# Token rows of a retention and mixture-of-experts kernel, moved into the quadrants of the matmul array

## The chip, the cores and the metric

One core of a Trainium2 chip runs the whole program. The metric is the device time of one launch in microseconds (us), lower is better. The kernel before took 1379.56 us in the median of three runs (1375.28 to 1381.71).

## What is computed

Eight batches of 576 tokens go through a retention layer with eight heads of 64 (scores, a decay mask by head, no softmax), then through eight experts, each token through the one with its largest gate product, and then through a second layer with a cosine. The reference, cut to what matters:

```python
ret = scale * np.matmul(q, k.transpose(0, 1, 3, 2)) * Dmat      # Dmat = gamma[h] ** (i - j), i >= j
x = np.matmul(ret, v)                     # (8, 8, 576, 64), then (4608, 512): a token's heads side by side
logits = x @ w_gate                       # (4608, 8)
expert_idx = np.argmax(logits, axis=1)
for e in range(8):
    mask = expert_idx == e
    out[mask] = gate_w[mask, None] * (np.maximum(x[mask] @ w1[e], 0.0) @ w2[e])
h = out @ w_in
result = (h * np.cos(h)) @ w_out
```

## The kernel before, in words

The program has three stages: attention with routing (to about 175 us), the experts, and the cosine layer. The change touches the first and the host's layout of two inputs.

The first stage walks 40 steps: eight batches, each in five chunks of tokens (four of 128, one of 64; `CH`). The loop `for i in range(NS)` emits instructions in the order in which the engines run them; there is no scheduler behind it, each engine works through its own list in order. The step numbers differ by function: step i does `scores(i)`, `decay(i + 1)`, `inter(i - 1)`, `intra(i - 1)` and `rows(i - 2)`.

- `load` (lines 438 to 441) brings transposed k and q, and v and k by rows: 1 MB for a full chunk, 384 KB for a half one. Five buffers; step i issues the load of step i + 4 on SyncE's queue, behind the store of token rows of that step.
- `decay` (L449) scales the values by head: eight ScalarE multiplications of 128x64 into `vs`.
- `scores` (L462): 16 TensorE matmuls of 64x64 weights by 128 columns, in the four quadrants of the array (two heads by two halves of the keys). VectorE multiplies the two PSUM banks by the causal mask into `pT` (L466).
- `inter` (L487) multiplies q by the sum carried from earlier chunks (`sbd`), `intra` (L497) the masked scores by the values; both add into `xps`. VectorE scales the sum into `xt` (L500). L506 adds the chunk to the carried sum, which ScalarE copies to `sbd` (L509).
- `rows` (L518) turns the transposed result into token rows and takes the gate products at once: four matmuls with 128x128 of `xt` as weights and 136 columns of `wgi`, an identity (128) beside the gate weights (8). ScalarE copies the rows to `xs` (L520), VectorE adds up two pairs' gate products (L521), and SyncE stores the rows to `xd` (L523).
- `route`, `place`, `spread` and `table` work once a batch: the token's expert (VectorE), its place among the expert's tokens (small matmuls L555 to L563), a one-hot spread on GpSimd (L575 to L626), and a matmul that enters it into the token table (L637). The GpSimd part begins in the third step of the next batch, and the table matmul stands behind `intra` three steps later.

In a trace a float32 matmul stands as two records, so 16 matmuls read x32. The scores, the rows and the turned expert inputs share four PSUM banks ("sc").

At the start, 13 bf16 matmuls on a blank tile (`warm`) come first. GpSimd makes the decay tables of chunks 1 to 4 (L399) and issues three small DMAs for the gate weights, from which `setup_rows` builds `wgi` on VectorE.

Of the kernel before, what the change touches and what calls it, by code (L numbers as in the profile page):

```python
# [22 lines left out]
P = 128  # L23
# [17 lines left out]
NWARM = 13  # L41

# [19 lines left out]
C_EYE = C_BASE + E  # L62
C_LO = C_EYE + E
# [5 lines left out]
def const_table(B):  # L69

    NT = B * SEQ
    t = np.zeros((P, C_END), np.float64)
    p = np.arange(P)
    t[:, C_ID:C_ID + 128] = np.eye(128)
    t[:, C_MASK:C_MASK + 128] = p[:, None] <= p[None, :]
    t[:, C_TRI:C_TRI + 128] = p[:, None] < p[None, :]
    t[:, C_ONE:C_ONE + 128] = 1.0
    t[:, C_IOTA:C_IOTA + 128] = p
    gam = 1.0 - 2.0 ** (-5.0 - np.arange(H))

    hp = 2 * np.arange(4)[None, :] + ((p >= D)[:, None] ^ (np.arange(4) % 2 == 1)[None, :])
    for c, (o, n) in enumerate(CH):
        pos = (o + p)[:, None] - CENTER
        t[:, C_GK + c * H:C_GK + (c + 1) * H] = gam[None] ** (-pos)
        t[:, C_GF + 4 * c:C_GF + 4 * c + 4] = gam[hp] ** o
        t[:, C_REV + c * E:C_REV + (c + 1) * E] = E - np.arange(E)
    t[:, C_GX:C_GX + 512] = (gam[hp][:, :, None] ** (p - CENTER)[None, None, :] / math.sqrt(D)).reshape(P, 512)
    t[0, C_BASE:C_BASE + E] = NT * np.arange(E)
    for j in range(4):
        t[32 * j:32 * j + E, C_EYE:C_EYE + E] = np.eye(E)  # L90
    t[:, C_B:C_B + MAXOVB] = np.arange(MAXOVB)
    t[:, C_E:C_E + E] = np.arange(E)
    t[:, C_WIN:C_WIN + E] = WIN
    for e in range(E):
        t[:, C_LO + e * NBLK:C_LO + (e + 1) * NBLK] = e * NT + P * np.arange(NBLK)
    for c in range(NBLK):
        t[:, C_SLOT + c] = c * P + p
    for b in range(B):
        for c, (o, n) in enumerate(CH):
            t[:, C_TOK + b * NCH + c] = b * SEQ + o + p  # L100
    return t.astype(np.float32)


def of_chunks(q, k, v):
# [13 lines left out]
    return full, np.concatenate([turned(k, o, n), turned(q, o, n)], axis=2), rows(v, o, n)  # L118


@with_exitstack
def attn_moe_kernel(ctx, tc, full, part, tail, wg, w1, w2, win, wout, ctab, out):
# [235 lines left out]
    with ExitStack() as actx:  # L358
# [16 lines left out]
        wgs = ap1.tile([P, 4, E], F32, name="wgs")  # L375

        RW = P + E
# [11 lines left out]

        def setup_rows():  # L390
            nc.vector.tensor_copy(out=wgi[:, 0::2, 0:P], in_=ident.unsqueeze(1).to_broadcast([P, 2, P]))
            for a in range(2):
                nc.vector.tensor_copy(out=wgi[:, 1::2, a * D:(a + 1) * D],
                                      in_=ident[:, (1 - a) * D:(2 - a) * D].unsqueeze(1).to_broadcast([P, 2, D]))
            nc.vector.tensor_copy(out=wgi[:, :, P:RW], in_=wgs)
# [47 lines left out]
        def decay(i):  # L443
            b, c = steps[i]
            o, n = CH[c]
            s = st[i]
            vs = ap3.tile([P, H, D], F32, tag="vs", name="vs", bufs=4) if n == P else halfv[b % 2]
            for h in range(H):
                nc.scalar.mul(vs[:n, h], s["v"][:n, h], cc(C_GK + c * H + h, 1, n))  # L449
            s["vs"] = vs  # L450
# [60 lines left out]
        def rows(i):  # L511
            b, c = steps[i]
            o, n = CH[c]
            x = ap3.tile([P, 4, P], F32, tag="xs", name="xs")
            for g in range(2):
                two = ps1.tile([P, 4, P], F32, tag="sc", name="rw", bufs=4).rearrange("p (j a) t -> p j (a t)", a=2)
                for j in range(2):
                    mm(out=two[:, j, 0:RW], lhsT=xts[i % 3][:, 2 * g + j, :], rhs=wgi[:, 2 * g + j, :], start=(j == 0),  # L518
                       stop=True, skip_group_check=True)
                nc.scalar.copy(out=x[:n, 2 * g:2 * g + 2], in_=two[:n, :, 0:P])  # L520
                nc.vector.tensor_reduce(out=lgt[b % 2][:n, c, g, :], in_=two[:n, :, P:RW].rearrange("p j e -> p e j"),  # L521
                                        axis=AX.X, op=ALU.add)
            nc.sync.dma_start(out=xd[b * SEQ + o:b * SEQ + o + n, :], in_=x[:n].rearrange("p j t -> p (j t)"))  # L523
# [175 lines left out]

        load(0, (0, 2))  # L700
        nc.sync.dma_start(out=ca[:, :C_TRI - C_MASK], in_=ctab[:, C_MASK:C_TRI])
        load(0, (2, 3))
        load(1, (0, 2))
        nc.sync.dma_start(out=gx[:, 0].rearrange("p j t -> p (j t)"), in_=ctab[:, C_GX:])
        load(0, (3, 4))
        load(1, (2, 4))
        load(2, (0, 2))
        nc.sync.dma_start(out=ct, in_=ctab[:, :C_MASK])
        load(2, (2, 4))
        load(3)  # L710
        wgc = wg.rearrange("(c p) e -> p c e", p=P)
        nc.gpsimd.dma_start(out=wgs[:, 0::2], in_=wgc[:, 0::2])
        for a in range(2):
            nc.gpsimd.dma_start(out=wgs[a * D:(a + 1) * D, 1::2], in_=wgc[(1 - a) * D:(2 - a) * D, 1::2])
# [4 lines left out]
        warm(NWARM, ps1.tile([P, 8, P], F32, tag="x", name="xps").rearrange("p a t -> p (a t)"), idle)  # L719
        decay(0)  # L720
# [3 lines left out]
        for i in range(NS):  # L724
# [6 lines left out]
            if i + 1 < NS:  # L731
                decay(i + 1)
            if i == 1:
                setup_rows()
# [13 lines left out]
            if i >= 2:  # L748
                rows(i - 2)
# [24 lines left out]

        inter(NS - 1)
        intra(NS - 1)
        rows(NS - 2)
# [656 lines left out]
```

## Time and profile before

| | |
|---|---|
| median of 3 runs | 1379.56 us |
| the profiled execution | 1377.58 us, its span 1375.3 us |
| TensorE busy (share of the span) | 1354.1 us (98%) |
| VectorE busy | 939.5 us (68%) |
| ScalarE busy | 757.2 us (55%) |
| GpSimd busy | 191.0 us (14%) |
| HBM traffic over the span | 217 GB/s |

Busy shares are means over three stages with different limits. A profile of a stage is read from windows of time, and a wait from the rows around it: a bracket behind a row says how long its engine stood idle before it and what released it.

### The profile page before, as it was taken

The page shows a single profiled execution, that of the slowest core. Times are in us where ns is not written, and L with a number is a line of the kernel's source. Part 1 is how long each engine was busy: PE and PEld are TensorE (multiplying, and loading weights), DVE is VectorE, ACT ScalarE, POOL GpSimd, SP SyncE. Part 2 cuts the span into 40 slices and gives each one's busy share as a digit, 9 for nine tenths or more (in the row PEclk, how much of TensorE's full clock was granted, in tenths as well). Part 3 has the DMA queues.
Part 4 walks back from the last instruction along what each step waited for, and adds up shares of the span by engine and source line. Part 5 has one row for each costly group of instructions (what it writes and reads, how often), then busy time and mean ns, then how long its engine had stood idle before and what let it go on. Part 6 is the DMA issues. An engine that isn't in the chain of part 4 may idle for free.

```text
span 1375.3 us, 28314 instructions
## 1 busy us (share of the span) xinstructions
PE 1354.1 (98%) x11234; PEld 1262.5 (92%) x11234; DVE 939.5 (68%) x1928; ACT 757.2 (55%) x1687; POOL 191.0 (14%) x300
## 2 busy tenths in 40 slices
PE   7999999999999999999999999999999999999998
PEld 6888899999999999998999999999999999999997
DVE  4777865867778687847666676766767676666655
ACT  5788725444544455336556555555555555555544
POOL 4334530121211212100010100101001010010101
PEclk9999999999999999999999999999999999999999
DMA  8899626575876668976564655646455564564551
GB/s 290 320 329 346 213 61 217 180 262 183 285 246 203 211 230 268 331 275 259 176 258 164 220 190 191 220 166 249 183 192 201 194 233 161 209 226 162 196 184 57
DMA packets 72648, 300.58 MB, mean 219 GB/s; under 512 B 7748, under 2 KB 15904, under 8 KB 58560
## 3 DMA queue, kind: packets, MB, share of 16 engines
q1 hardware_dynamic: 60000, 256.18, 53.0%
q0 software_dynamic: 12512, 42.56, 8.3%
q8 instruction: 89, 1.46, 0.4%
q14 instruction: 47, 0.39, 0.1%
HBM read 247.24 MB, written 51.47 MB: 217 GB/s over the span
## 4 chain that ended last, share of the span: by engine, by line
PE 49%; issue 6%; POOL 0%; POOLq 0%; ACT 0%
PE acc L1341 25%; PE hps L1265 24%; POOL out_dram L1323 0%; POOLq L1430 0%; ACT ka L1295 0%; POOL spare L159 0%; PE acc L1352 0%; POOLq L1323 0%; ACT orow L1321 0%
## 5 line engine op out<-in xcount | busy, mean ns | idle before, releaser
L1341 PE MATMUL acc<-wunit,gh 128*128 128x512 f32 x1152 | 358.2, 392 | 0.0
L1265 PEld LDWEIGHTS hps<-far,wquad 128*128 128x128 f32 x2064 | 261.8, 191 | 8.0 <-ACTq L1239 0.7
L1265 PE MATMUL hps<-far,wquad 128*128 128x256 f32 x2064 | 266.7, 283 | 0.5 <-ACTq L1239 0.5
L1341 PEld LDWEIGHTS acc<-wunit,gh 128*128 128x128 f32 x1152 | 207.2, 189 | 36.0
L1341 PE MATMUL acc<-wunit,gl 128*128 128x512 f32 x576 | 224.3, 389 | 0.0
L274 PE MATMUL hps<-xT,wunit 128*128 128x256 f32 (+6 forms) x1536 | 209.4, 297 | 0.5 <-ACT yev L291 0.5
L274 PEld LDWEIGHTS hps<-xT,wunit 128*128 128x128 f32 x1536 | 206.7, 188 | 0.9 <-ACT yev L291 0.7
L289 PE MATMUL hps<-hh,wunit 128*128 128x256 f32 (+6 forms) x960 | 197.9, 301 | 0.0
L289 PEld LDWEIGHTS hps<-hh,wunit 128*128 128x128 f32 x960 | 155.8, 190 | 0.1
L289 PE MATMUL hps<-hl,wunit 128*128 128x256 f32 (+6 forms) x480 | 143.5, 299 | 1.4 <-DVE hl L278 1.4
L1323 POOL DMA_INDIRECT out_dram<-orow,perm x36 | 35.4, 982 | 740.3 <-DVE orow L1319 736.4
L1341 PEld LDWEIGHTS acc<-wunit,gl 128*128 128x128 f32 x576 | 108.2, 188 | 24.5 <-DVE gl L1308 0.8
L1306 ACT CAST gh<-sa 128x512 fp32r<-128x512 f32 x144 | 89.6, 622 | 72.9 <-DVE sa L1302 72.9
L1302 DVE SCALAR_TENSOR_TENSOR sa<-sa,box 128x512 f32<-128x512 f32 x144 | 99.0, 688 | 42.8 <-ACT sa L1300 41.7
L1265 PE MATMUL hps<-near,wquad 128*128 128x256 f32 x960 | 126.6, 283 | 0.0
L1265 PEld LDWEIGHTS hps<-near,wquad 128*128 128x128 f32 x960 | 123.1, 191 | 3.6
L1276 DVE TENSOR_TENSOR box<-hps,box 128x256 f32<-128x256 f32 x72 | 30.6, 424 | 136.7 <-PE hps L1265 136.5
L1308 DVE TENSOR_TENSOR gl<-sa,gh 128x512 fp32r<-128x512 f32 x144 | 98.9, 687 | 18.5 <-ACT gh L1306 12.9
L1297 DVE SCALAR_TENSOR_TENSOR sa<-box,ka 128x512 f32<-128x512 f32 x144 | 98.9, 687 | 12.4 <-ACT ka L1295 12.3
L1275 ACT COPY box<-hps 128x256 f32<-128x256 f32 x72 | 26.8, 372 | 141.3 <-PE hps L1265 132.5
L1021 DVE TENSOR_TENSOR wunit<-wst,wunit 128x512 fp32r<-128x512 f32 x112 | 75.2, 686 | 36.9 <-ACT wunit L1020 36.8
L1299 ACT ACTIVATE sa<-sa 128x512 f32<-128x512 f32 x144 | 91.2, 634 | 8.6 <-DVE sa L1297 8.6
(217 smaller groups left out, 1877.4 us busy)
## 6 DMA issues: line engine op xcount, KB each, us to landing
wquad<-ws SPq DMA_DIRECT2D x72, 1792.0 KB
wst<-in_moe_w_dram SPq DMA_DIRECT2D x64, 512.0 KB
ld<-in_full_dram SPq DMA_DIRECT2D x29, 1024.0 KB
ws<-cvo POOLq DMA_DIRECT2D x28, 512.0 KB, 3.5
xd<-xs SPq DMA_DIRECT2D x32, 256.0 KB
cvw<-in_moe_w_in_dram SPq DMA_DIRECT2D x16, 512.0 KB
cvw<-in_moe_w_out_dram SPq DMA_DIRECT2D x16, 512.0 KB
wd<-cvo POOLq DMA_DIRECT2D x16, 512.0 KB, 5.3
```

What stands on the lines that cost most here:

```text
L274: mm(out=ph[:, :n], lhsT=u[:, a, kc, f0:f0 + P], rhs=t[:, bq, kc, :n], start=(idx == 0), stop=(idx == 11))
L289: mm(out=py[:, :n], lhsT=u[:, w], rhs=t[:, :n], start=(fc == 0 and g == 0), stop=(fc == 7 and g == 2))
L1021: nc.vector.tensor_sub(out=u[:, 1, 2 * g + c], in0=s[:, c], in1=u[:, 0, 2 * g + c])
L1265: mm(out=o, lhsT=u[:, s, kc, a], rhs=x[:, bq, kc], start=(s in (0, 1, 2) and idx == 0), stop=(idx == 5), skip_group_check=True)
L1276: nc.vector.tensor_add(out=u2, in0=y[:, :HT], in1=p1)
L1297: nc.vector.scalar_tensor_tensor(out=sa, in0=x, scalar=INV2PI, in1=ka, op0=ALU.mult, op1=ALU.subtract)
L1299: nc.scalar.activation(out=sa, in_=sa, func=AF.Sin, scale=math.pi)
L1302: nc.vector.scalar_tensor_tensor(out=sa, in0=sa, scalar=-1.0, in1=x, op0=ALU.add, op1=ALU.mult)
L1306: nc.scalar.copy(out=gh, in_=sa)
L1308: nc.vector.tensor_sub(out=gl, in0=sa, in1=gh)
L1323: ins = nc.gpsimd.indirect_dma_start(out=out[:, :], out_offset=bass.IndirectOffsetOnAxis(ap=perm[:, k:k + 1], axis=0), in_=o, in_offset=None)
L1341: mm(out=acc2[T][c], lhsT=pair[n][:, fh, c % 2 * P:(c % 2 + 1) * P], rhs=u[:, w, fc % 4], start=(q == 0 and fh == 0 and n == 0 and w == 0) ...
```

## The change

`rows` uses the array in quadrants: for each of four head pairs, two halves of the features and two halves of the tokens, one matmul of 64x64 by 72 columns (64 of an identity, 8 of gate weights); a PSUM bank now holds one half of the features for all four pairs, so a gate product adds four numbers instead of two. It is emitted between `scores` and `inter` of a step, no longer behind `intra`. The gate table with its identities comes from the host in one DMA on SyncE's queue; `setup_rows` and the three small DMAs go. The tokens' features change order within odd pairs, and the host orders the gate's and w1's rows to match.

`decay`: in the first three steps one VectorE multiplication of 128x512 does all heads, emitted behind the step's own scores; from step 3 on ScalarE does heads 0 to 3 one by one and GpSimd heads 4 to 7 in one multiplication. At the start a ScalarE multiplication of one element comes first (it brings the table load forward), the loads are reordered, and six more warming matmuls stand behind the first scores.

```diff
+def of_gate(w):
+    t = w.reshape(4, 2, D, E).copy()
+    t[1::2] = t[1::2, ::-1]
+    out = np.zeros((2, D, 4, RW), w.dtype)
+    out[:, :, :, :D] = np.eye(D)[:, None, :]
+    out[:, :, :, D:] = t.transpose(1, 2, 0, 3)
+    return out.reshape(P, 4 * RW)
...
-            for h in range(H):
+            h0 = 0 if i < OWN else H // 2
+            for h in range(h0):
                 nc.scalar.mul(vs[:n, h], s["v"][:n, h], cc(C_GK + c * H + h, 1, n))
+            (nc.vector if i < OWN else nc.gpsimd).tensor_tensor(
+                out=vs[:n, h0:], in0=s["v"][:n, h0:],
+                in1=cc(C_GK + c * H + h0, H - h0, n).unsqueeze(2).to_broadcast([n, H - h0, D]), op=ALU.mult)
...
         def rows(i):
-            x = ap3.tile([P, 4, P], F32, tag="xs", name="xs")
+            xt = xts[i % 3]
+            x = ap3.tile([P, 4, 2, D], F32, tag="xs", name="xs")
+            two = [ps1.tile([P, 4, P], F32, tag="sc", name="rw", bufs=4).rearrange("p j t -> p (j t)")[
+                :, :4 * RW].rearrange("p (j f) -> p j f", f=RW) for g in range(2)]
+            for j in range(4):
+                for g, r in ((0, 0), (1, D), (0, D), (1, 0)):
+                    if r < n:
+                        mm(out=two[g][r:r + D, j, :], lhsT=xt[D * g:D * g + D, j, r:r + D],
+                           rhs=wgi[D * g:D * g + D, j, :], start=(j == 0), stop=True, skip_group_check=True)
             for g in range(2):
-                two = ps1.tile([P, 4, P], F32, tag="sc", name="rw", bufs=4).rearrange("p (j a) t -> p j (a t)", a=2)
-                for j in range(2):
-                    mm(out=two[:, j, 0:RW], lhsT=xts[i % 3][:, 2 * g + j, :], rhs=wgi[:, 2 * g + j, :], start=(j == 0),
-                       stop=True, skip_group_check=True)
-                nc.scalar.copy(out=x[:n, 2 * g:2 * g + 2], in_=two[:n, :, 0:P])
-                nc.vector.tensor_reduce(out=lgt[b % 2][:n, c, g, :], in_=two[:n, :, P:RW].rearrange("p j e -> p e j"),
+                nc.scalar.copy(out=x[:n, :, g, :], in_=two[g][:n, :, 0:D])
+                nc.vector.tensor_reduce(out=lgt[b % 2][:n, c, g, :], in_=two[g][:n, :, D:RW].rearrange("p j e -> p e j"),
                                         axis=AX.X, op=ALU.add)
...
+        nc.scalar.mul(spare, one[0:1], one[0:1])
         load(0, (0, 2))
         nc.sync.dma_start(out=ca[:, :C_TRI - C_MASK], in_=ctab[:, C_MASK:C_TRI])
+        load(1, (0, 2))
         load(0, (2, 3))
-        load(1, (0, 2))
+        load(0, (3, 4))
         nc.sync.dma_start(out=gx[:, 0].rearrange("p j t -> p (j t)"), in_=ctab[:, C_GX:])
-        load(0, (3, 4))
         load(1, (2, 4))
         load(2, (0, 2))
+        nc.sync.dma_start(out=wgi.rearrange("p c e -> p (c e)"), in_=wg)
...
-        decay(0)
...
             scores(i)
-            if i + 1 < NS:
+            if i < OWN:
+                decay(i)
+            if i == 0:
+                warm(NWARM // 2, blank, idle)
+            if OWN <= i + 1 < NS:
                 decay(i + 1)
-            if i == 1:
-                setup_rows()
+            if i >= 2:
+                rows(i - 2)
...
             if i >= 1:
                 inter(i - 1)
                 intra(i - 1)
...
-            if i >= 2:
-                rows(i - 2)
```

TensorE's list in the third step, before: scores, carried sum (`sbd`), within the chunk (`pT`, `vs`), sum `S`, rows (`rw`), and the next scores.

```order
L462 MATMUL sc<-ld 64x128 x16
L487 MATMUL xps<-ld,sbd_136 64x128 x8
L497 MATMUL xps<-pT,vs 64x128 x8
L506 MATMUL S<-vs,ld 64x64 x8
L518 MATMUL rw<-wgi,xt_130 128x136 x4
```

The same step after the change:

```order
L474 MATMUL sc<-ld 64x128 x16
L533 MATMUL rw<-wgi,xt_129 64x72 x16
L499 MATMUL xps<-ld,sbd_135 64x128 x8
L509 MATMUL xps<-pT,vs 64x128 x8
L518 MATMUL S<-vs,ld 64x64 x8
```

The rows moved from the step's end to behind its scores, and four matmuls became 16.

GpSimd's list around a batch's spread, before (`dd`, `hot`, `rt`, `oh` lead to the token table):

```order
L584 TENSOR_TENSOR dd<-dd,hot 128x200
L608 TENSOR_SCALAR tokc<-ct 128x5
L609 TENSOR_TENSOR rt<-hot,tokc 128x5x40
L612 TENSOR_SCALAR oh<-ca,rm 128x128 x5
L626 TENSOR_TENSOR rt<-hot,gh 128x5x40
L626 TENSOR_TENSOR rt<-hot,gl 128x5x40
```

And after, where `vs` and `halfv` are the scaled values:

```order
L600 TENSOR_TENSOR dd<-dd,hot 128x200
L459 TENSOR_TENSOR halfv_142<-ld,ca 64x256
L624 TENSOR_SCALAR tokc<-ct 128x5
L625 TENSOR_TENSOR rt<-hot,tokc 128x5x40
L628 TENSOR_SCALAR oh<-ca,rm 128x128 x5
L642 TENSOR_TENSOR rt<-hot,gh 128x5x40
L642 TENSOR_TENSOR rt<-hot,gl 128x5x40
L459 TENSOR_TENSOR vs<-ld,ca 128x256 x4
```

One multiplication now stands in the middle of the chain and four stand between one batch's chain and the next.

## Rows read from the trace of the kernel before

**Rows 1.** The page: busy time by engine, and the chain that ended last
```profile
PE 1354.1 (98%) x11234; PEld 1262.5 (92%) x11234; DVE 939.5 (68%) x1928; ACT 757.2 (55%) x1687; POOL 191.0 (14%) x300
...
PE 49%; issue 6%; POOL 0%; POOLq 0%; ACT 0%
```
**Rows 2.** Windows: length, busy PE, PEld, DVE, ACT, POOL, granted clock, DMA share, GB/s
```profile
0.00:21.23 21.23, 13.41 (x198) 10.79 (x198) 6.04 (x16) 9.85 (x36) 14.97 (x32) 0.92 0.86 294
89.99:109.78 19.79, 19.54 (x405) 17.68 (x404) 15.73 (x47) 16.54 (x59) 8.52 (x16) 1.00 0.92 326
109.78:129.48 19.70, 19.70 (x406) 17.75 (x405) 15.72 (x47) 16.31 (x59) 8.34 (x15) 1.00 0.96 351
129.48:148.97 19.49, 19.49 (x406) 17.70 (x405) 15.92 (x51) 16.18 (x59) 8.14 (x15) 1.00 0.88 306
...
85.00:90.00 5.00, 5.00 (x92) 4.43 (x88) 4.30 (x14) 4.18 (x14) 4.67 (x9) 1.00 1.04 406
...
166.00:1375.30 1209.30, 1198.92 (x8121) 1123.88 (x8121) 823.82 (x1578) 632.24 (x1236) 121.87 (x177) 1.00 0.58 206
```
**Rows 3.** Timeline, one full step, weight loads: start, us, engine, line, operation, [idle before]
```profile
102.04 0.86 PEld L462 LDWEIGHTS sc<-ld 64*64 64x64 f32 x32
102.86 0.48 PEld L487 LDWEIGHTS xps<-ld,sbd 64*64 64x64 f32 x16
103.51 0.85 PEld L497 LDWEIGHTS xps<-pT,vs 128*64 128x64 f32 x16 [0.17 <-issue]
105.00 0.99 PEld L518 LDWEIGHTS rw<-wgi,xt 128*128 128x128 f32 x8
106.12 0.20 PEld L462 LDWEIGHTS sc<-ld 64*64 64x64 f32 x4
```
**Rows 4.** Timeline of TensorE at a half chunk
```profile
110.71 0.41 PE L487 MATMUL xps<-ld,sbd 64*64 64x64 f32 x16
111.05 0.69 PE L497 MATMUL xps<-halfpT,halfv 128*64 128x64 f32 x16
111.68 0.55 PE L637 MATMUL lg<-rt,oh 128*128 128x120 f32 x3
```
**Rows 5.** Timeline of one spread on GpSimd; a table matmul a batch earlier
```profile
102.98 0.52 POOL L575 TENSOR_TENSOR dd<-dsts,ca 128x200 f32<-128x200 f32 x1 [10.85 <-DVE dsts L569]
...
110.17 0.53 POOL L626 TENSOR_TENSOR rt<-hot,gh 128x200 fp32r<-128x200 f32 x1
110.65 0.97 POOL L626 TENSOR_TENSOR rt<-hot,gl 128x200 fp32r<-128x200 f32 x1
...
92.19 0.91 PE L637 MATMUL lg<-rt,oh 128*128 128x120 f32 x5 [0.25 <-POOL rt L626]
```
**Rows 6.** Timeline of the start, TensorE and ScalarE
```profile
1.15 2.95 PE L211 MATMUL xps<-idle 128*128 128x256 bf16 x13 [1.15 <-DVE idle L718]
9.88 1.98 PE L462 MATMUL sc<-ld 64*64 64x128 f32 x32 [3.44 <-DMA ld<-in_full_dram]
18.02 0.67 PE L487 MATMUL xps<-ld,sbd 64*64 64x128 f32 x16 [2.68 <-ACT sbd L509]
...
8.51 1.28 ACT L449 ACT_TABLE_LOAD   x1 [8.51 <-DMA ld<-in_full_dram]
...
18.98 2.02 ACT L449 ACTIVATE vs<-ld,ca 128x64 f32<-128x64 f32 x8 [1.01 <-DMA ld<-in_full_dram]
```
**Rows 7.** Waits (20 to 166 us), the long stall, VectorE by form, a DMA queue
```profile
ACT vs L449 <- DMA ld<-in_full_dram: 13.6, 12, 3.6
...
60.46 1.78 ACT L449 ACTIVATE vs<-ld,ca 128x64 f32<-128x64 f32 x7 [3.57 <-DMA ld<-in_full_dram]
60.85 0.39 PE L506 MATMUL S<-vs,ld 128*64 128x64 f32 x6 [1.67 <-issue]
...
L500 DVE TENSOR_TENSOR xt<-xps,gx 128x512 f32<-128x512 f32 x13 | 8.8, 676 | 0.0
...
q8 instruction: 22, 0.36, 1.1%
```

More of the change, by code (lines that the diff above doesn't have):

```diff
@@ L41 @@
 NWARM = 13
+OWN = 3
 INV2PI = 1.0 / (2.0 * math.pi)
@@ L61 @@
 C_BASE = C_REV + NCH * E
-C_EYE = C_BASE + E
-C_LO = C_EYE + E
+C_LO = C_BASE + E
 C_IOTA = C_LO + E * NBLK
@@ L88, in const_table @@
     t[0, C_BASE:C_BASE + E] = NT * np.arange(E)
-    for j in range(4):
-        t[32 * j:32 * j + E, C_EYE:C_EYE + E] = np.eye(E)
     t[:, C_B:C_B + MAXOVB] = np.arange(MAXOVB)
@@ L118, in of_chunks, with of_first @@
     return full, np.concatenate([turned(k, o, n), turned(q, o, n)], axis=2), rows(v, o, n)
+RW = D + E
+def of_gate(w):
[5 more added lines that the diff above has]
+    return out.reshape(P, 4 * RW)
+def of_first(w):
+    t = w.reshape(E, 4, 2, D, F1).copy()
+    t[:, 1::2] = t[:, 1::2, ::-1]
+    return t.reshape(E, DM, F1)
 @with_exitstack
@@ L374, in attn_moe_kernel @@
         rbase2 = ap1.tile([P, E], BF16, name="rbase2")
-        wgs = ap1.tile([P, 4, E], F32, name="wgs")
-        RW = P + E
         wgi = ap1.tile([P, 4, RW], F32, name="wgi")
@@ L388, in setup_ranking @@
             nc.vector.memset(rsb, 0.0)
[L390 to L395, printed above, removed]
         def decay_table(c):
@@ L513, in rows @@
             o, n = CH[c]
-            x = ap3.tile([P, 4, P], F32, tag="xs", name="xs")
-            for g in range(2):
-                two = ps1.tile([P, 4, P], F32, tag="sc", name="rw", bufs=4).rearrange("p (j a) t -> p j (a t)", a=2)
-                for j in range(2):
-                    mm(out=two[:, j, 0:RW], lhsT=xts[i % 3][:, 2 * g + j, :], rhs=wgi[:, 2 * g + j, :], start=(j == 0),
-                       stop=True, skip_group_check=True)
-                nc.scalar.copy(out=x[:n, 2 * g:2 * g + 2], in_=two[:n, :, 0:P])
-                nc.vector.tensor_reduce(out=lgt[b % 2][:n, c, g, :], in_=two[:n, :, P:RW].rearrange("p j e -> p e j"),
+            xt = xts[i % 3]
[7 more added lines that the diff above has]
+                           rhs=wgi[D * g:D * g + D, j, :], start=(j == 0), stop=True, skip_group_check=True)
+            for g in range(2):
+                nc.scalar.copy(out=x[:n, :, g, :], in_=two[g][:n, :, 0:D])
+                nc.vector.tensor_reduce(out=lgt[b % 2][:n, c, g, :], in_=two[g][:n, :, D:RW].rearrange("p j e -> p e j"),
                                         axis=AX.X, op=ALU.add)
-            nc.sync.dma_start(out=xd[b * SEQ + o:b * SEQ + o + n, :], in_=x[:n].rearrange("p j t -> p (j t)"))
+            nc.sync.dma_start(out=xd[b * SEQ + o:b * SEQ + o + n, :], in_=x[:n].rearrange("p j g d -> p (j g d)"))
         def cst(col, c0, n):
@@ L710, in attn_moe_kernel @@
         load(3)
[L711 to L714, printed above, removed]
         for c in range(1, NCH):
@@ L718, in attn_moe_kernel @@
         nc.vector.memset(idle, 0.0)
-        warm(NWARM, ps1.tile([P, 8, P], F32, tag="x", name="xps").rearrange("p a t -> p (a t)"), idle)
-        decay(0)
+        blank = ps1.tile([P, 8, P], F32, tag="x", name="xps").rearrange("p a t -> p (a t)")
+        warm(NWARM, blank, idle)
         wq = dict(zip((6, 7, 11, 15, 16, 21, 25, 26), [(key, g) for key in w_units(0) for g in range(2)]))
@@ L773, in attn_moe_kernel @@
                 unit_load(ap3, *wq[i])
+        rows(NS - 2)
         inter(NS - 1)
         intra(NS - 1)
-        rows(NS - 2)
         table(*waiting.pop())
@@ L1418 @@
     laid = dict(zip(("full", "part", "tail"), of_chunks(inputs['q'], inputs['k'], inputs['v'])))
+    laid["moe_w_gate"] = of_gate(inputs["moe_w_gate"])
+    laid["moe_w1"] = of_first(inputs["moe_w1"])
     for name in ["full", "part", "tail"] + _INS:
```

## The prediction, made before the changed kernel was run

> **What bounds the kernel now.** I read, in this order, the busy totals and the chain, the windows by stage, one step of the first stage in time, the waits there, and the start. The totals say TensorE is busy 98% of the span [rows 1], and the chain is almost only TensorE. That is an average: the change touches the stage that ends near 175 us, and behind it TensorE is busy 1198.9 of 1209.3 us [rows 2]. So time won in that stage should arrive at the end whole, since every engine's later program simply begins earlier; this holds unless the stage itself gives it back.
>
> Inside it, look at the windows. A batch is five steps, and I cut the windows at the start of scores, so their lengths are times of the program: scores 3 start at 21.23, and three batches from the middle take 19.79, 19.70 and 19.49 us [rows 2]. TensorE is busy in practically all of each. But the DMA share in them is 0.92, 0.96 and 0.88 and VectorE is busy 15.7 to 15.9 us: three resources lie close together, so a gain on TensorE can't be handed on one for one.
>
> **Part 1, rows() on TensorE.** Before, one step issues 16 score matmuls, 8 for the carried sum, 8 within the chunk, 8 for the sum and 4 of 128x128 by 136 columns for rows. In the full step that I use, rows start at 105.00 and the next scores at 106.12: 1.12 us [rows 3]. The change issues 16 matmuls of 64x64 by 72 columns, spread over the four quadrants. No such row exists, so I bound it by two that use the quadrants. Scores, 16 of 128 columns, take 0.82 us from 102.04 to the next weight load at 102.86 [rows 3]; by columns that is 0.82 x 72/128 = 0.46. The half chunk's carried sum, 8 of 64 columns, takes 0.34 us from 110.71 to 111.05, with the change of array shape in it [rows 4]; times 2.25 that is 0.77. I take 0.54: nearer the first, which has the same 16 instructions in the same order of quadrants. The saving lies between 1.12 - 0.77 = 0.35 and 1.12 - 0.46 = 0.66.
>
> Where rows stand matters too. Weight loads idle 0.17 us as "issue" when 64-row matmuls give way to 128-row ones [rows 3]. Rows now stand between two users of quadrants and meet no such edge, but the step still has one from sums to scores, of which a few hundredths stay outside the 1.12. So I take a saving of 0.55 a step. The Trainium skill, "TensorEngine Tiling (Array Packing)", Tiling Modes, says that a change of tiling mode drains the array. The trace agrees with an edge of 0.17 us; if the surviving edge cost that in full on top, the saving would be 1.12 - 0.54 - 0.17 = 0.41, and the sum below, worked out in the same way, 9.9 instead of 13.3 us.
>
> From step 3 on, 39 of 40 rows() run where TensorE never stands still: 39 x 0.55 = 21.5 us if TensorE alone sets the pace.
>
> **Part 2, half the values on GpSimd.** ScalarE issues four of its eight multiplications, some 1 us less a step (8 take 2.02 us [rows 6]). ScalarE is not what ends, so this is worth nothing by itself. GpSimd gets 37 multiplications of 256 elements. GpSimd rows of 200 elements with two inputs take 0.52, 0.53 and 0.97 us [rows 5]; by size 0.67 to 1.24. I take 0.7, as two of the three lie there. One stands ahead of the token table's chain. That chain runs from 102.98 to 111.62 (8.65 us) and TensorE's table matmul starts at 111.68, right behind it; a batch earlier TensorE even waits 0.25 us for it [rows 5]. There is no slack left. The change lengthens the chain by 0.7 us, and takes cover away: two old rows() lay between place and table (2 x 1.12), three new ones will (3 x 0.54), so TensorE arrives 0.6 us sooner. The new wait is 0.7 + 0.6 = 1.3 us a batch. By itself that turns 19.7 - 5 x 0.55 = 16.95 into 18.2 us a batch.
>
> **Part 3, DMA under it.** A batch that also loads expert weights moves 351 GB/s x 19.70 us = 6.9 MB at share 0.96. Taken as pure occupancy its floor is 18.9 us; at the best 5 us slice, 406 GB/s [rows 2], it is 17.0. The last full window, without weights, has 6.0 MB: 14.7 to 17.2. So 18.2 us lies inside these bounds and I let it stand for all batches: a gain of 1.5 us each, with DMA able to take back 0.7 of it in a weight batch.
>
> **Part 4, the start.** Scores 1 wait 3.44 us for their load, ScalarE loads its table only when values land (8.51) and multiplies step by step, and the first carried sum waits 2.68 us for ScalarE [rows 6]. The reordered loads, the early table load and three multiplications on VectorE (0.68 us each by a row of 512 elements [rows 7]) remove the ScalarE part. What is late next is load 3: ScalarE gets it at 18.98 [rows 6]. The new gate table adds about 0.13 MB ahead of it, 0.4 us at 294 GB/s [rows 2]; scores 3 then start near 19.4 instead of 21.23 [rows 2]. That is 1.8 us, between 0 and 2.7 (the carried sum's wait). Six more warming matmuls lie in a wait for DMA and cost nothing; if that cover went, by the 13 in 2.95 us [rows 6] they'd cost 1.4. The four DMAs of the old gate weights and VectorE's three copies leave idle time, nothing. Host layouts leave the later loads alike.
>
> **The sum.** Start 1.8, steps 3 and 4 2 x 0.55 = 1.1, six batches 6 x 1.5 = 9.0, and the last six rows() 3.3, less one table wait of 1.3 and 0.6 of the wait that stands by the last transposes: 1.4. Total 13.3. The profiled execution took 1377.6 (span 1375.3 and 2.3 around it), so 1364.3; the median shown is 2.0 above it and would give 1366.3. I forecast 1365.0. A measurement here tells about 0.5%, 6.9 us, from no change.
>
> **Rivals.**
> *TensorE sets the pace alone.* The table wait vanishes (VectorE's part of the chain comes sooner), DMA keeps up and the one long stall, 3.57 us of ScalarE on a load and 1.67 of TensorE [rows 7], goes too: 1.8 + 21.5 + 2.2 = 25.5, 1352 to 1354. For it: DMA moved 406 GB/s in a slice. Against: VectorE's 15.7 us in 16.95 leaves it 93% busy with waits of its own. Chance 0.20.
> *DMA is the bound already.* ScalarE waits 13.6 us in 12 places for loads [rows 7]. If weight batches can't go under 18.9, and TensorE's extra instructions (56 matmuls a step for 44) add to the instruction fetches (22 packets, 1.1% of the DMA engines' time, in 140 us [rows 7]), a batch costs about 19.2: 2.9 + 6 x 0.5 + 1.4 = 7.3, so 1370 to 1372. Chance 0.17.
> *GpSimd becomes the bound: slower.* Place: the table chain. TensorE tolerates a chain of 8.05 us (8.65 less 0.6); the new one is 9.35. A batch is slower than before once the wait exceeds the 2.75 won, from 10.8 us; with the start's 2.9 and the end's 1.4 spread over seven tables from 11.4, which is GpSimd 22% slower than I assume. Its last product took 0.97 us where the one before, as large, took 0.53 [rows 5], so it happens to single instructions. With the whole chain at 1.5 times, 14.0 us, a wait is 5.95: six batches lose 3.2 each, the end 5.95 + 0.6 - 3.3, the start wins 2.9, together 19.6 more, near 1398. Chance 0.05. The Trainium skill, "GPSIMD Engine Reference", Key points, has elementwise work about twice as slow there as on VectorE, and contention when VectorE reads two SBUF inputs. By the first, estimated from VectorE's 0.68 us for 512 elements [rows 7], a multiplication would be 0.68 and this rival no nearer; whether the second made the slow product slow, no row here shows.
> *The change doesn't do what it says: the quadrants don't overlap.* Then 16 x 72 columns go one after another: at scores' 0.82 us per 16 x 128, times 4, 1.85 us against 1.12, 39 x 0.73 = 28 us on TensorE, 1402 to 1407 by what the start gives. Scores in the trace speak against it. Chance 0.02.
> My forecast, with waits anywhere between the first two rivals: 0.56.
>
> **Numbers.** The range reaches from the first rival to just past the second, 1352 to 1376. Faster: 0.56 + 0.20 and a fifth of the DMA case, 0.79. Same: the rest of that case, 0.14. Slower: the last two, 0.07.
>
> **What would show it.** Right: about 0.5 us from a step's scores to its carried sum beyond the 0.82, batches near 18 us, the table matmuls behind GpSimd's last product by about 1.3 us, scores 3 near 19.4. Wrong: batches at 17.0 with no table wait (first rival), loads waited for in each step (second), or batches over 19.7.

## Result, and the profile after

The changed kernel took 1397.76 us in the median of four runs, the kernel before 1378.4 us beside it: ratio 1.0123, 95% interval 1.0099 to 1.0147. The forecast was 1365.0 (1352 to 1376), so it missed on the wrong side: slower by 1.2%.

The profiled execution took 1399.08 us, its span 1397.3. I cut it at the same places of the program as before (the start of the scores of a step, the first expert matmul, the first matmul of the cosine layer):

| piece | before, us | after, us | difference |
|---|---|---|---|
| to scores 3 | 21.23 | 19.59 | -1.64 |
| scores 3 to scores 5 | 7.74 | 12.25 | +4.51 |
| six batches, scores 5 to scores 35 | 120.00 | 128.07 | +8.07 |
| scores 35 to scores 39 | 16.94 | 19.62 | +2.68 |
| scores 39 to the first expert matmul | 7.95 | 10.69 | +2.74 |
| experts | 436.7 | 441.6 | +4.9 |
| cosine layer, to its last matmul | 758.7 | 758.6 | -0.1 |

The first stage alone is 16.4 us longer. The 4.9 us of the experts are no work of the change: their code is the same in all runs below, they took 438.7 to 442.7 us in the twelve others that compute the same (the kernel before with other scores 441.6), and the profile of before was on the low side there.

The page of the changed kernel, busy totals and the chain; they answer to [rows 1] and look just as good:

```profile
PE 1348.8 (97%) x12072; PEld 1258.3 (90%) x12072; DVE 944.0 (68%) x1927; ACT 713.6 (51%) x1516; POOL 210.9 (15%) x334
...
PE 48%; issue 5%; POOL 0%; POOLq 0%; ACT 0%
```

The windows of the changed kernel (columns as in [rows 2]): the start, three batches from the middle, 5 us behind the start, the stages behind the first:

```profile
0.00:19.59 19.59, 12.20 (x227) 9.57 (x228) 6.63 (x14) 1.97 (x4) 12.10 (x27) 1.00 0.85 298
98.26:120.10 21.84, 18.45 (x511) 16.90 (x509) 15.47 (x47) 11.08 (x38) 10.64 (x19) 0.92 0.80 290
120.10:140.17 20.07, 17.32 (x512) 15.86 (x508) 16.21 (x48) 11.18 (x38) 8.44 (x16) 1.00 0.89 311
140.17:159.91 19.74, 17.34 (x513) 15.84 (x509) 16.27 (x48) 11.06 (x38) 10.15 (x18) 1.00 0.81 287
20.00:25.00 5.00, 4.19 (x84) 3.49 (x77) 2.56 (x7) 3.04 (x12) 2.70 (x5) 0.50 0.84 294
190.22:1397.30 1207.08, 1193.32 (x8005) 1118.47 (x8004) 816.84 (x1550) 628.27 (x1228) 115.19 (x163) 1.00 0.58 206
```

The second and third batch have 17.3 us of TensorE work, 2.2 to 2.4 less than before, and still take 19.7 to 20.1 us. TensorE, busy in practically all of such a window before, now stands still for 2.4 to 3.4 us in each. No other resource took its place: VectorE is busy 15.5 to 16.3 us, about as before, and the DMA share fell to 0.80 to 0.89. So the work was saved and time lost elsewhere. The list of TensorE's waits between 20 and 182 us (total, times, longest) says on what:

```profile
PE sc L474 <- issue: 11.4, 7, 2.6
PE rw L533 <- issue: 10.3, 6, 2.4
PE S L518 <- issue: 1.9, 2, 1.1
PE rw L533 <- DVE xt L512: 0.8, 1, 0.8
```

The first three rows are fifteen pauses, 23.6 us, put down to "issue": TensorE waited for nothing that the list of waits shows. In the timeline of one and a half steps:

```profile
66.09 1.10 PE L474 MATMUL sc<-ld 64*64 64x128 f32 x32
67.01 0.68 PE L533 MATMUL rw<-wgi,xt 64*64 64x72 f32 x32
67.51 0.62 PE L499 MATMUL xps<-ld,sbd 64*64 64x128 f32 x16
68.06 1.09 PE L509 MATMUL xps<-pT,vs 128*64 128x128 f32 x16
68.98 0.63 PE L518 MATMUL S<-vs,ld 128*64 128x64 f32 x16
69.55 0.62 PE L474 MATMUL sc<-ld 64*64 64x64 f32 x13
72.23 0.33 PE L474 MATMUL sc<-ld 64*64 64x64 f32 x3 [2.06 <-issue]
```

The first step is what was forecast: the rows take 0.50 us (67.01 to 67.51), the step 3.46 (66.09 to 69.55). Then TensorE stops among 16 like matmuls, 13 records in, with three left, for 2.06 us. The kernel before has one such pause of note, [1.67 <-issue] at 60.85 [rows 7].

Where they fall tells what they are. Counted in the trace in matmul records from the program's start, the pauses begin at 350, 476, 603, 857, 983, 1364, 1490, 1871, 2124, 2378: apart by 126, 127, 254, 126, 381 and so on, always a multiple of about 127 records, whatever line they hit. Each record has a weight load beside it, so that is some 254 instructions of TensorE. Queue q8, "instruction", moves in packets of 16 KB, and between 20 and 166 us there are 27 of them (23 before); TensorE's 6679 records in that stretch (5862 before) make 26.3 (23.1) times 254. From 75.74 to 76.80 us one of them passes (packets, MB, share):

```profile
q8 instruction: 1, 0.02, 6.0%
```

It ran from 75.74 to 76.76 us; TensorE had stopped at 76.27, again inside a line, and went on at 78.22. The Trainium skill, "Runtime: NRT & Kernel Launch", Instruction fetch mechanics, has the sequencer fetch instructions by a DMA queue of its own in blocks of 16 KiB, 256 instructions; the spacing of the pauses agrees. It also says that the cost of crossing a block is mostly hidden, and there this trace disagrees, with 23.6 us.

That packet is no single case. The summary table below counts 101 pauses. Packets come some 5 us apart, and all pauses but one end 1.0 to 1.7 us after the end of a packet of q8; the pause of the kernel before that ends at 60.85 is among them (its packet ends at 59.35). The exception is a pause of 0.27 us in the kernel before. So it is the packet that TensorE waits for.

My theory A: TensorE runs out of instructions. The change issues 16 small matmuls for 4 large ones and shortens the step, so a block is used up sooner, and blocks share the DMA engines with loads. Rivals: B, GpSimd's half of the values delays something; C or P, the new place of the rows costs; D, a block costs its pause whatever the DMA engines do.

### The profile page after: what moved, and what is told of

It is laid out like the page before. It is cut to its first block, busy times and chain, and to the rows that moved or that the text cites. A ratio compares the mean times of both kernels' runs of the same rounds, so it can differ in the third digit from the quotient of the medians.

```text
span 1397.3 us, 29906 instructions
## 1 busy us (share of the span) xinstructions
PE 1348.8 (97%) x12072; PEld 1258.3 (90%) x12072; DVE 944.0 (68%) x1927; ACT 713.6 (51%) x1516; POOL 210.9 (15%) x334
## 4 chain that ended last, share of the span: by engine, by line
PE 48%; issue 5%; POOL 0%; POOLq 0%; ACT 0%
PE acc L1357 25%; PE hps L1281 23%; POOL out_dram L1339 0%; POOLq L1448 0%; ACT ka L1311 0%; POOL spare L177 0%; PE acc L1368 0%; POOLq L1339 0%; ACT orow L1337 0%
## 5 line engine op out<-in xcount | busy, mean ns | idle before, releaser
L1324 DVE TENSOR_TENSOR gl<-sa,gh 128x512 fp32r<-128x512 f32 x144 | 99.0, 687 | 18.2 <-ACT gh L1322 12.7
```

Of the source, the lines that this page charges most:

```text
L1324: nc.vector.tensor_sub(out=gl, in0=sa, in1=gh)
```

## The experiments

A summary first. Pauses are TensorE's waits put down to "issue", clock is the mean granted clock of TensorE, both between 20 and 182 us; six batches are scores 5 to scores 35 of the profiled run. Matmuls a step are the program's, a full chunk's. All but the ratio come from one profiled execution of each kernel; that of e5 took 1384.8 us, the shortest of its four, that of e4 1406.36, the longest.

| kernel | matmuls a step | six batches, us | pauses, us (times) | clock | ratio to before, 95% |
|---|---|---|---|---|---|
| before | 44 | 120.0 | 1.9 (2) | 1.00 | 1 |
| changed | 56 | 128.1 | 23.6 (15) | 0.92 | 1.0123 (1.0099 to 1.0147) |
| e1 full rows, new place | 44 | 121.5 | 0.6 (2) | 1.00 | 1.0037 (1.0024 to 1.0049) |
| e2 no GpSimd half | 56 | 136.5 | 23.4 (13) | 0.86 | 1.0221 (1.0201 to 1.0241) |
| e3 quadrant rows, old place | 56 | 140.4 | 27.0 (17) | 0.90 | 1.0162 (1.0128 to 1.0196) |
| e4 before, scores split | 60 | 145.6 | 12.7 (11) | 0.96 | 1.0128 (1.0102 to 1.0154) |
| e5 rows in halves | 48 | 118.4 | 1.4 (2) | 0.98 | 1.0082 (1.0055 to 1.0108) |
| e6 rows, scores in halves | 40 | 116.9 | 1.7 (4) | 0.98 | 1.0015 (1.0001 to 1.0029) |
| e7 no loads | 56 | 105.6 | 0 | 0.96 | not compared |
| e8 before, scores in halves | 36 | 120.5 | 0 | 1.00 | 1.0016 (1.0001 to 1.0030) |
| e9 full rows, old place | 44 | 119.0 | 0.2 (1) | 1.00 | 0.9984 (0.9962 to 1.0005) |
| e10 changed, ends late | 56 | 132.4 | 25.7 (15) | 0.93 | 1.0129 (1.0093 to 1.0165) |
| e11 e5, ends late | 48 | 120.1 | 2.9 (3) | 0.97 | 1.0033 (1.0015 to 1.0051) |
| e12 e6, ends late | 40 | 116.1 | 1.9 (2) | 1.00 | 0.9978 (0.9958 to 0.9997) |
| e13 quadrant rows, scores in halves | 48 | 126.4 | 13.4 (14) | 0.95 | 1.0029 (1.0010 to 1.0047) |

**e1, the rows as four full matmuls in the new place**

```diff
-                for g, r in ((0, 0), (1, D), (0, D), (1, 0)):
-                    if r < n:
-                        mm(out=two[g][r:r + D, j, :], lhsT=xt[D * g:D * g + D, j, r:r + D], ...
+                    mm(out=two[:, j, 0:RW], lhsT=xt[:, 2 * g + j, :], rhs=wgi[:, 2 * g + j, :], ...
```

> The changed kernel with one part undone: the token rows and gate products again as 4 matmuls of the full 128x128 array a step (they keep their new place between the scores and the carried sums, and GpSimd keeps half of the values). Theory A, instructions run out: TensorE stands still because the blocks that carry its instructions come too late; 12 matmuls a step less means a block every 5 to 6 us as in the kernel before, so the pauses that wait for nothing (15 of them, 23.6 us, in the changed kernel) fall to 0 to 3, stage 1 takes a step about 4.0 us again, and the time is 1370 to 1382 us. Theory B, half the values on GpSimd delay the table or the sums: that stays, so 1390 to 1400 us. Theory C, the new place of the rows is at fault: that stays too, 1390 to 1400 us.

1384.64 us. The pauses are gone and the clock with them is whole, which bears out A and speaks against B. But that is not all: 1.0037, some 2.6 us over A's range. What is left in TensorE's waits is new:

```profile
PE rw L531 <- DVE xT L278: 1.8, 1, 1.8
PE rw L531 <- DVE xt L512: 1.4, 1, 1.4
```

Both are rows that now stand ahead of the carried sum and wait for VectorE, in the last and in the fourth step; and a batch takes 20.3 us with TensorE busy all through, so the full matmuls cost more between users of quadrants. Theory P is that the new place costs in these ways; e9 to e12 take it up.

**e2, no GpSimd half; e3, the quadrant rows at the step's end**

```diff
-            h0 = 0 if i < OWN else H // 2
-            for h in range(h0):
-                nc.scalar.mul(vs[:n, h], s["v"][:n, h], cc(C_GK + c * H + h, 1, n))
...
+            else:
+                for h in range(H):
+                    nc.scalar.mul(vs[:n, h], s["v"][:n, h], cc(C_GK + c * H + h, 1, n))
```

> The changed kernel with the scaled values all on ScalarE again from the fourth step on (quadrant rows and their place kept). Theory A (instructions run out): TensorE's instructions are the same, so 12 or more pauses that wait for nothing stay, and the time stays at 1390 to 1402 us. Theory B (GpSimd's half of the values): 1365 to 1380 us, with the pauses gone.

```diff
-            if i >= 2:
-                rows(i - 2)
             if i >= 1:
                 inter(i - 1)
                 intra(i - 1)
...
+            if i >= 2:
+                rows(i - 2)
```

> The changed kernel with the quadrant rows put back to the end of a step, behind the carried sums, as they stood before. Theory A: as many instructions, so the pauses stay (12 or more) and the time is 1390 to 1402 us. Theory C (the new place, which sets when PSUM tiles and the rows' store come free): 1365 to 1382 us. Theory B: 1390 to 1402 us too.

1409.59 and 1403.26 us. The pauses stay in both, 23.4 and 27.0 us, so neither B nor the place makes them. Both lie above the 1402 us that A allowed, and e2 is clearly slower than the changed kernel, which no theory had said; e3's interval overlaps the changed kernel's. The granted clock is lower too, 0.86 and 0.90 for 0.92, while e2's pauses add up to no more than the changed kernel's. GpSimd's half is thus a help here, not a harm. Why as much idle time costs more clock in e2 was not settled.

**e4, the kernel before with each score matmul cut in two**

```diff
-                        mm(out=scs[g][r:r + D, j, :n], ...
+                        for c0 in (0, n // 2):
+                            mm(out=scs[g][r:r + D, j, c0:c0 + n // 2], ...
```

> The kernel before with every score matmul cut into two of half the columns: 16 more matmuls a step (60 for 44) with the same columns in all, nothing else changed. Theory A: TensorE's pauses that wait for nothing, of which the kernel before has one in stage 1, become 10 or more, and its granted clock falls to half in stretches behind them, as in the changed kernel; time 1395 us or more. Theories B and C: neither GpSimd nor the place of the rows is touched, so no such pauses; the time grows by the extra weight loads alone, from nothing to 16 x 0.03 us x 39 steps = 19 us, without a fall of the clock.

1398.8 us. This is the kernel before with more instructions for the same columns, and it shows the changed kernel's pauses, eleven on four lines:

```profile
PE sc L463 <- issue: 4.4, 4, 1.7
PE xps L489 <- issue: 3.8, 4, 1.8
PE rw L520 <- issue: 2.8, 1, 2.8
PE S L508 <- issue: 1.7, 2, 1.3
```

The 25.6 us of six batches are more than the pauses: the extra matmuls and their weight loads cost too, as the expectation allowed for: in the batch from 78.31 to 99.81, with one pause of 0.2 us, TensorE is busy for 21.3 us, where batches of the kernel before have 19.5 to 19.7 [rows 2]. The pauses and the clock are what tells the theories apart.

**e7, the changed kernel without the loads of seven batches**

```diff
+            if b > 0:
+                s.update({key: st[c][key] for key in ("ld", "kT", "qT", "v", "k")})
+                return
```

> The changed kernel without the loads of q, k and v of the second to the eighth batch: these batches compute on the first batch's tiles, so the output is another one and only stage 1 is to be read. TensorE's instructions and their order are those of the changed kernel. Theory A (the block of instructions waits behind the loads in the DMA engines): with some 35 MB of the 50 MB of stage 1 gone, pauses fall from 15 to 0 to 3 and the last scores of stage 1 start at 150 to 158 us instead of 179.5 us. Theory D (a block costs its pause whatever the DMA engines do): 12 or more pauses stay, last scores at 170 us or later. Theory B (GpSimd half of the values, table): pauses stay.

The instructions are the same, and the pauses are gone: in the list of waits between 20 and 182 us nothing is left on "issue". The first row is what stands there instead, six table matmuls waiting 0.7 us each for GpSimd:

```profile
PE lg L656 <- POOL rt L645: 4.2, 6, 0.7
```

The six batches of both kernels as windows, first the changed one, then the one without loads:

```profile
31.84:159.91 128.07, 108.29 (x3048) 98.87 (x3044) 95.46 (x283) 65.83 (x226) 62.59 (x108) 0.95 0.83 301
```

```profile
29.39:135.00 105.61, 101.16 (x3048) 92.57 (x3045) 94.39 (x283) 64.81 (x226) 62.66 (x106) 1.00 0.34 111
```

The same 3048 matmul records take 105.61 us with the DMA engines a third full and 128.07 with them at 0.83. Of the difference 7.1 us are busy time (the clock is 0.95 for 1.00) and 15.3 idle time. The last scores start at 149.72, just before the 150 to 158 expected; the time of the whole run, 1683.91 us with another output, isn't compared. So D falls: it isn't the crossing of a block that costs but a block that comes late, because the loads are in the way.

The packets tell more. A packet of q8 passes in 1.0 to 1.1 us on average in both kernels, so the loads don't slow it on its way; it starts later. I count from the moment when TensorE began the block before the one that the packet brings. Without the loads the packet starts at most 1.7 us after that (29 to 150 us). In the six batches of the changed kernel, packets that start 0.0 to 2.7 us after it leave no pause or one below 1 us, and those that start 3.0 to 4.4 us after it leave pauses of 1.0 to 2.6 us. Where it doesn't pause and has the full clock, the changed kernel uses up a block in 4.0 to 4.7 us. The kernel before takes 5.4 us or more (60 to 166 us), and there packets that start up to 3.7 us after that moment cost no pause. What holds a packet before its start, the records don't tell; a row of the same kind is the store of token rows (`xd`, 256 KB), whose median from issue to landing is 5.4 us in the changed kernel and 2.0 without loads, between 20 and 166 us.

**e5, e6 and e8, matmuls over half of the array's rows**

The rows (e5), rows and scores (e6), or in the kernel before the scores (e8):

```diff
-                for g, r in ((0, 0), (1, D), (0, D), (1, 0)):
-                    if r < n:
-                        mm(out=two[g][r:r + D, j, :], lhsT=xt[D * g:D * g + D, j, r:r + D], ...
+                for g in range(2):
+                    mm(out=two[g][:n, j, :], lhsT=xt[D * g:D * g + D, j, :n], ...
```

> The changed kernel with the rows as 8 matmuls a step instead of 16: each takes 64 partitions and all 128 tokens as weights (one half of the array's rows, all its columns), two of them side by side, the same columns of output in all. 48 matmuls a step (changed kernel 56, before 44). Theory A (instructions run out, a block serves about 63 matmuls of the program): fewer blocks by a seventh, so pauses fall from 23.6 us to 5 to 15 us, and the time to 1372 to 1388 us; if the halves do not run side by side the rows cost 0.5 us a step more and it is 1385 to 1395 us. Theory D (fetching a block always costs TensorE its 1.5 us, however far apart blocks are): pauses fall by a seventh only, 20 us, and the time is 1390 to 1396 us.

> The changed kernel with rows and scores both as 8 matmuls over half of the array's rows and all its columns: 40 matmuls a step, fewer than the 44 of the kernel before. Theory A: a block lasts a step and a half, 5.4 us or more, as long as before; 0 to 4 pauses in stage 1 and 1355 to 1372 us, under the kernel before. Theory D: 9 to 11 pauses of 1.5 us stay, 1380 to 1392 us. If halves do not run side by side: no pauses, but 1 us a step more, 1385 to 1400 us.

> The kernel before with the scores alone as 8 matmuls over half of the array's rows (36 matmuls a step for 44). Theory A: the kernel before has one pause in stage 1, so there is next to nothing to win: 1374 to 1381 us, pauses 0 or 1. If halves do not run side by side, 0.4 to 0.8 us a step more: 1393 us or more.

1390.4, 1381.25 and 1382.47 us. With 48 or 40 matmuls a step the pauses all but go, far more than the seventh that D allows. (By its time alone e5 would fit D's range too, and the 1385 to 1395 us for halves that don't run side by side.) But halves are dearer in TensorE's own time than I had reckoned. In e12 (below), rows in halves, 86.98 to 87.93, take 0.95 us where quadrants take 0.50 in the timeline above, and scores 0.99 for 0.92:

```profile
85.99 1.16 PE L473 MATMUL sc<-ld 64*128 64x128 f32 x16
86.98 1.01 PE L531 MATMUL rw<-wgi,xt 64*128 64x72 f32 x16
87.93 0.46 PE L498 MATMUL xps<-ld,sbd 64*64 64x64 f32 x16
```

In halves a matmul takes about 0.12 us, with 72 columns as with 128. The weight loads beside them are busy for 0.98 and 0.97 us in the trace and may set that pace, which no run tests. So e5 and e6 stayed above the 1388 and 1372 us that A allowed. And e8, 1.5 us above its range, says that saved matmuls alone win nothing where TensorE wasn't short of them.

**e9, the rows wholly as before; e10, e11, e12, the rows late in the fourth and the last step**

e9 is e1 with the rows behind `intra`. The other three are the changed kernel, e5 and e6 with

```diff
-            if i >= 2:
+            if i >= 2 and i not in (3, NS - 1):
                 rows(i - 2)
...
+            if i in (3, NS - 1):
+                rows(i - 2)
```

> The changed kernel with the rows wholly as before: 4 matmuls of the full array and at the step's end. What is left of the change is the start, the order of the loads and GpSimd's half of the values. The run with full rows in the new place took 1.0037 of the kernel before, with six batches in the middle at 20.3 us against 20.0. Theory P (the new place costs: an edge between array shapes more in a step, a wait for the copied transposes at the stage's end, a wait for xt in the fourth step): the wait at the end falls from 1.8 us to under 1, middle batches return to 19.8 us or less, and the time is 1374 to 1379 us. Theory B (GpSimd's half costs): batches stay at 20.2 us or more and the time is 1382 to 1387 us.

> The changed kernel with the rows late (behind the carried sums) in two steps only, the fourth and the last, early in all others. Theory P for the ends: the 2.7 us that rows wait for the copied transposes go to under 1, and so do the half clock behind it (2.3 us lost in the two blocks after it) and the 0.8 us of the fourth step: 4 to 6 us less than the changed kernel, 1391 to 1394 us, with the pauses in the middle as they were (12 or more). Rival: the pauses lie elsewhere then and take it back, 1396 us or more.

> The changed kernel with the rows as 8 matmuls over half of the array's rows (48 a step) and late in the fourth and the last step. With rows early throughout it took 1.0082 of the kernel before, with 2.2 us of wait for the transposes and half the clock from 20 to 30 us. Theory A and P: no long pauses after 60 us, wait at the end under 1, so 1376 to 1384 us. Rival (pauses merely shift): 1386 us or more.

> The changed kernel with rows and scores as 8 matmuls each over half of the array's rows (40 a step) and the rows late in the fourth and the last step. With rows early throughout it took 1.0015 of the kernel before, with 2.3 us of wait for the transposes and about 2.5 us of half clock behind it. Theory A and P: both go, no pause in stage 1, 1371 to 1377 us, the kernel before beaten by 0.1 to 0.6%. Rival: what is won in stage 1 is given back behind it, 1378 to 1383 us.

1379.38, 1396.71, 1385.73 and 1377.06 us. e9 against e1 is theory P, with the time 0.4 us above its range: six batches 119.0 for 121.5 us, the wait for `xT` 0.5 for 1.8. What the new place costs at the stage's end is seen in the changed kernel's timeline: rows wait 2.73 us, and the matmuls behind them run at half the clock (16 records in 1.97 us that take 1.09 at 68.06):

```profile
183.07 0.66 PE L533 MATMUL rw<-wgi,xt 64*64 64x72 f32 x27 [2.73 <-DVE xT L278]
...
184.44 1.97 PE L509 MATMUL xps<-pT,vs 128*64 128x128 f32 x16
```

With the ends late the piece from scores 39 to the experts falls from 10.69 to 7.29 us (e10), 9.90 to 7.83 (e11) and 12.78 to 7.96 (e12). In e10 nothing of that arrives: six batches took 132.4 us, with 25.7 us of pauses, the rival's case. e11, 1.7 us above its range, and e12, 0.1 us above its own and with two pauses left for none, keep it: 1.0082 became 1.0033 and 1.0015 became 0.9978. e12 thus ends at 0.9978 of the kernel before, interval 0.9958 to 0.9997: faster by 0.2% than the kernel before, in an interval that just leaves out 1. In its fullest batches TensorE is busy throughout and DMA close to it:

```profile
85.99:104.91 18.92, 18.92 (x385) 17.34 (x381) 15.74 (x48) 11.05 (x38) 10.91 (x20) 1.00 0.97 356
104.91:124.00 19.09, 19.09 (x384) 17.51 (x381) 16.38 (x48) 11.04 (x38) 11.13 (x20) 1.00 0.98 339
```

**e13, quadrant rows kept, the matmuls saved in the scores**

```diff
-                for g, r in ((0, 0), (1, D), (0, D), (1, 0)):
-                    if r < n:
-                        mm(out=scs[g][r:r + D, j, :n], lhsT=s["kT"][D * g:D * g + D, j, r:r + D], ...
+                for g in range(2):
+                    mm(out=scs[g][:n, j, :n], lhsT=s["kT"][D * g:D * g + D, j, :n], ...
```

> The changed kernel with its quadrant rows (16 matmuls a step) kept, the scores as 8 matmuls over half of the array's rows (so 48 a step for 56), and the rows late in the fourth and the last step. In the runs before, scores in halves took 1.0 to 1.2 us a step (quadrants 0.92) and rows in halves 0.95 (quadrants 0.50), so a step by itself is 3.6 to 3.7 us, 13 to 13.5 matmuls a us. Runs at 12.2 a us (48 a step, 3.95 us) had four pauses in stage 1, at 14.7 (60 a step) ten, at 16.2 fifteen. Theory A with a supply that depends on the rate alone: 4 to 9 pauses, 6 to 14 us, and 1374 to 1386 us. Theory A with a block that is late only when it must come within 4 us: no more than 4 pauses, 1368 to 1375 us, the fastest kernel of this study. Rival, quadrant rows cost something of their own beside their number: 1388 us or more.

1383.3 us, in the range of a supply that depends on the rate alone, if with more and shorter pauses than I said (14 for 4 to 9, 13.4 us):

```profile
PE rw L532 <- issue: 8.9, 7, 1.8
PE sc L473 <- issue: 1.9, 3, 1.2
```

It has as many matmuls a step as e5 and e11, but a shorter step (3.68 us for 3.92, 13.0 matmuls a us for 12.2), so it asks for them faster, and it pauses where they hardly do. So the number a step doesn't decide, and quadrant rows aren't needed for pauses, since e4 has them without. The rate does, but not alone: e4 asks for some 14.5 a us and pauses no longer than e13, under a DMA share of 0.78 for e13's 0.88 (20 to 166 us). A faster TensorE meets this limit sooner.

## Why the prediction was wrong, point by point

**Part 1, rows() on TensorE: right.** 0.50 us a full step against 0.54 forecast, the step 3.46 for 4.08 [rows 3], a saving of 0.62 for 0.55. Where the trace has the loads out of the way (e7), three batches take 17.93, 17.94 and 18.06 us (scores at 81.07, 99.00, 116.94 and 135.00), against 18.2 forecast by parts 1 and 2 together.

```profile
81.07:99.00 17.93, 17.04 (x513) 15.55 (x509) 16.11 (x48) 10.96 (x38) 11.29 (x20) 1.00 0.29 99
```

**Where rows stand: mis-sized.** I counted only the edge between array shapes. The new place also puts rows ahead of the carried sum, so that TensorE meets two waits for VectorE that the sums had covered: 0.81 us for `xt` in the fourth step and 2.73 us for `xT` in the last, where the kernel before waits 0.56 for `xT`. With the clock behind the second that makes the 2.7 us lost ahead of the experts.

**Part 2, GpSimd: right in kind, too dear.** The multiplication takes 0.61 to 0.66 us for 0.7. The table wait is 0.7 us a batch (e7) for 1.3, and in the changed kernel there is none, since TensorE comes late. The rival that ended slower, GpSimd, is refuted by e2: without its half the kernel is slower still.

```profile
113.62 0.61 POOL L459 TENSOR_TENSOR halfv<-ld,ca 64x256 f32<-64x256 f32 x1
...
118.51 0.52 POOL L642 TENSOR_TENSOR rt<-hot,gl 128x200 fp32r<-128x200 f32 x1
```

The chain's last product, the one of 0.97 us before [rows 5], took 0.52 here.

**Part 3, DMA under it: the step that failed.** It priced DMA by bytes, 17.0 to 18.9 us a batch, and let the batch stand at 18.2 since it lay between. The rival "DMA is the bound already" had the instruction fetches, but as occupancy too, 1.1% of the DMA engines' time [rows 7]. Occupancy is not what they cost: a packet of 1 us, if late, stops TensorE wherever it is. The sum took it for granted that TensorE begins an instruction as soon as its semaphores allow, and so put the supply of instructions at nothing. In its place the runs show 23.6 us of pauses in the first stage and a clock of 0.92: six batches lost 8.1 us where the sum had a gain of 9.0. 56 matmuls in 3.46 us are 16.2 a us, where the kernel before asks for 44 in about 4.0, 11. The forecast's own number, 56 for 44, was the warning, and the row was there: the 1.67 us "issue" of TensorE at 60.85 [rows 7], in the middle of a line. I put it down to one long load stall that might go, and did not ask what is missing for an engine whose semaphores are all there.

**Part 4, the start: right, then lost.** Scores 3 start at 19.59 against 19.4 forecast, 1.64 us won, and what they wait for is their load, as forecast. But TensorE waits for loads and for xt in that stretch, and its granted clock from 20 to 25 us is 0.50, the lower of its two levels (1.2 for 2.4 GHz), where it was 1.00 before. A pause of 1.60 us follows:

```profile
19.62 1.70 PE L474 MATMUL sc<-ld 64*64 64x128 f32 x32 [2.13 <-DMA ld<-in_full_dram]
22.13 1.24 PE L533 MATMUL rw<-wgi,xt 64*64 64x72 f32 x32 [0.81 <-DVE xt L512]
...
29.05 0.33 PE L474 MATMUL sc<-ld 64*64 64x64 f32 x4 [1.60 <-issue]
```

By scores 5 the kernel is 2.9 us behind. e7 has like waits and the lower clock there too, but no pause, and takes 10.1 us from scores 3 to scores 5, where the changed kernel takes 12.25 and the kernel before 7.74. So about half of that loss came with the pause. The sum had no term for clock. The kernel before had its own stretch at the lower level earlier, at scores 1 (32 records in 1.98 us [rows 6] that take 1.10 in the changed kernel), so part of the 1.64 us is clock too.

**The sum.** 13.3 us were to be won; the first stage lost 16.4. In the middle, e7's 105.6 us and the changed kernel's 128.1 differ by 22.5 us: the pauses and the clock behind them, less the 4.2 us that e7 waits for its tables instead. The gain of rows exists only as long as TensorE is fed.

## What to carry to other kernels

Before large matmuls are cut into small ones, count matmuls per microsecond beside TensorE's time: here 9 to 12.2 a us ran almost free under a DMA share of 0.87 to 0.90 (20 to 166 us), and 13 or more under 0.78 to 0.88 did not. An "issue" pause inside a run of like instructions is a row to stop at; if such pauses lie a fixed number of instructions apart, look for an instruction packet that ends just ahead of each pause's end, as here. In these runs a faster step made the pauses more. When work moves ahead of other work in an engine's list, look at what that other work was covering, at the first and the last steps above all.

## What was not expected of the hardware

- Pauses of 0.2 to 3.4 us at multiples of about 127 matmul records (some 254 instructions), seen in every kernel with 13 or more matmuls a us and loads beside them; without the loads the same instruction list has none after 20 us. A pause ends 1.0 to 1.7 us after the packet of instructions has passed.
- Short idle times can cost more than their length: with 23 to 27 us of pauses in the stage the granted clock of TensorE fell to 0.86 to 0.93 of the whole, with under 3 us it stayed at 0.96 to 1.00 (e7's 0.96 stands by its waits for loads and VectorE at the two ends of the stage). In the changed kernel four of the six stretches at the lower level begin at a pause of 1.9 to 2.6 us or just behind it (at 54.1, 95.1, 115.6 and 163.3 us), but pauses of 2.0 us at 70.16, 76.27 and 141.41 have none behind them. Kernels with the same pauses (23.4 and 23.6 us in e2 and the changed one) differ by 8.4 us in six batches; their clocks, 0.86 and 0.92, differ with it, and why was left open.
- Two matmuls over half of the array's rows each do not share it as four quadrants do: rows in halves 0.95 us, in quadrants 0.50, with the same columns of output. With 128 columns the difference is small: scores 0.99 and 0.92.
